# Moving all GpSimd arithmetic of a fused attention and two-layer kernel to VectorE

## The chip, the cores and the metric

One core of one Trainium2 chip runs the whole program. The metric is device time in microseconds (us) of one execution, the median of three runs. Times of single instructions and waits come from one profiled execution.

## The reference

Everything is float32. Three stages follow each other.

```python
# 1 attention, q, k, v: 4 batches, 8 heads, 576 positions, 64 wide
q_d, k_d, v_d = means over groups of 4 positions            # 144 positions
out_up = repeat(softmax(q_d k_d^T / 8) v_d, 4)
out_local = softmax(where(|i - j| < 4, q k^T / 8, -1e9)) v   # a narrow band
x = (out_up + out_local)  as 2304 tokens x 512
# 2 first gated layer, 512 -> 1536 -> 512
x = ((x @ w_a) * (x @ w_b)) @ w_out
# 3 second gated layer, 512 -> 2048 -> 512
h = x @ w_in
x = (h * clip(h + 3, 0, 6) / 6) @ w_out2
```

The softmax sums have 1e-9 added before the division.

## The kernel before

The weights arrive as 64-bit words, and the kernel turns each word into float32 itself. `decode` (line 229) does that for one tile of 128 x 1024 words in a buffer `raw`: ScalarE takes a magnitude (L243), VectorE runs six instructions (L249, L250, L254, L260, L261, L267), and then the value is split into a coarse part and a remainder, so that TensorE can multiply in three passes (`PASSES`) in its quick format. The coarse part is ScalarE's copy (`first`, L271). The remainder is a subtraction (`second`, L275), on VectorE where `soon` is set (the first three tiles of the first layer's weights), else on GpSimd. There are 12 tiles `wab` (first layer, w_a and w_b together), 6 tiles `wo`, 8 tiles `w2i` and 8 tiles `w2o`. Two `raw` buffers exist, and the subtraction frees one for the next load.

`pieces` (line 292) decodes a `w2i` tile, forms seven combinations of its quarters (L308), copies each to its place (L317) and subtracts (L321). Its flag `soon` is set for tiles 5 to 7. For tiles 0 to 4 GpSimd subtracts.

The attention goes in two forms. `pooled` (line 361) takes one pair of heads of one batch: sums of four positions of q and k (VectorE, L391), sums of v (`add_v`, L386 and L387, on GpSimd), scores (TensorE, L400), maxima (VectorE, L405 and L408), exponentials with their sums (ScalarE, L414), reciprocals (VectorE, L420 and L421), the normalisation (`scaled`, L353), a transposition (TensorE, L432) and the product with v (L447). `local` (line 470) takes one unit of 116 tokens and all heads of a batch in the same steps (L487/L493, L501/L502, L509, L514/L515, L353, L524, L536), adds the two results (VectorE, L544) and splits x into coarse part and remainder (ScalarE L551, VectorE L554). The normalisation L353 is VectorE's for block 0 (the flag `first`, `m < 1`) and GpSimd's for all else.

The 20 units form seven blocks of tokens (`BLOCKS`). `job` (line 562) multiplies one block with one `wab` tile: 12 matmuls for a, 12 for b (L586), ScalarE copies a out of PSUM (L592), VectorE multiplies by b (L595), and SyncE stores to DRAM (L598). There are 84 jobs. Then come the second product of layer one (`second`, L643, with h loaded, copied at L631 and subtracted at L635), and layer two (`inner`, L755; `outer`, L878).

Nothing is put in order by hand. `Plan` keeps a list of steps with engine, estimated length, the time at which each is wanted, dependencies and buffers taken and given, walks through them as a clock would, and writes each instruction when its engine is free, its inputs are there and its buffers are free; of several, the one wanted first. So each engine's queue is fixed when the program is written, and an engine that waits for one instruction holds up all behind it. A step's engine and length (lines 185 to 202) decide where everything else lands.

Of the kernel before, what the change touches and what calls it, by code (L numbers as in the profile page):

```python
# [138 lines left out]
def fused_kernel(ctx: ExitStack, tc: tile.TileContext, qk, vt, vd, wab, wo, w2i, w2o, mask, out):  # L139
# [54 lines left out]
    def act(n):  # L194
        return 0.1 + 0.00095 * n

    def pool(n):
        return 0.2 + 0.0023 * n

    def dma(kb):  # L200
        return 0.0039 * kb

# [8 lines left out]
    def DVE(busy, want, run, after=(), take=(), give=(), slack=0.0):  # L211
        return plan.add("DVE", busy, want, run, after, take, give, DVE_L + slack)

    def POOL(busy, want, run, after=(), take=(), give=(), slack=0.0):
        return plan.add("POOL", busy, want, run, after, take, give, DVE_L + slack)

    issued = {}

    def DMA(kb, want, run, after=(), take=(), give=()):
# [6 lines left out]
    wab_t, wo_t, w2_t = {}, {}, {}  # L226
    pools = {}

    def decode(src, want, put, tag, after=(), ahead=4, soon=False, slack=1.0, raw=None, queue=None):

        T = {}

        def load():
            T["raw"] = slot(xp if raw == "x" else dp, [P, W], mybir.dt.uint64, raw or "raw", "raw")
            (queue or nc.sync).dma_start(T["raw"], src)

        def words():
            w = T["raw"].bitcast(U32).rearrange("p (n t) -> p n t", t=2)
            return w[:, :, 0], w[:, :, 1]

        def magnitude():
            T["m"] = slot(dp, [P, W], F32, "dm", "m")
            nc.scalar.activation(T["m"], words()[1].bitcast(F32), AF.Abs)  # L243

        def exponent():
            m = T["m"]
            mu = m.bitcast(U32)

            nc.vector.tensor_scalar(m, m, W_MIN, W_MAX, op0=ALU.max, op1=ALU.min)  # L249
            nc.vector.tensor_scalar(mu, mu, 3, 0x3FFFFFF8, op0=ALU.logical_shift_left, op1=ALU.bitwise_and)  # L250

        def upper():
            hi = words()[1]
            nc.vector.scalar_tensor_tensor(out=hi, in0=hi, scalar=0xC0000000, in1=T["m"].bitcast(U32),  # L254
                                           op0=ALU.bitwise_and, op1=ALU.bitwise_or)

        def lower():
            m, (lo, hi) = T["m"], words()

            nc.vector.tensor_scalar(m.bitcast(U32), hi, 0xFF800000, None, op0=ALU.bitwise_and)  # L260
            nc.vector.scalar_tensor_tensor(out=lo.bitcast(F32), in0=lo, scalar=2.0 ** -52, in1=m,  # L261
                                           op0=ALU.mult, op1=ALU.mult)

        def both():
            lo, hi = words()
            v = hi.bitcast(F32)
            nc.vector.tensor_tensor(v, v, lo.bitcast(F32), op=ALU.add)  # L267

        def first():
            T["w"] = put()  # L270
            nc.scalar.activation(T["w"][:, 0], words()[1].bitcast(F32), AF.Copy)  # L271

        def second():
            eng = nc.vector if soon else nc.gpsimd
            eng.tensor_tensor(T["w"][:, 1], words()[1].bitcast(F32), T["w"][:, 0], op=ALU.subtract)  # L275


        i = DMA(1024, want - ahead, load, take=[raw or "raw"])
        i = ACT(act(W), want, magnitude, [i], take=["dm"], slack=slack)
        i = DVE(2 * dve2(W), want, exponent, [i])  # L280
        i = DVE(dve(W), want, upper, [i])
        i = DVE(dve2(W) + dve(W), want, lower, [i], give=["dm"])
        if put is None:
            return DVE(dve(W), want, both, [i], slack=slack), words
        i = DVE(dve(W), want, both, [i], slack=slack)
        i = ACT(act(W), want, first, [i, *after], take=[tag], slack=slack)
        return (DVE(dve(W), want, second, [i], give=[raw or "raw"]) if soon else
                POOL(pool(W), want, second, [i], give=[raw or "raw"]))

    takers = {}  # L290

    def pieces(src, want, where, soon, raw=None):


        i, words = decode(src, want, None, None, slack=1.0, raw=raw)
# [17 lines left out]
        for at, of, q, n in ((0, 0, 0, 2), (2, 0, 3, 1), (3, 1, 0, 4)):  # L313
            for a, b, key, tag, before, place in where(at, at + n):
# [3 lines left out]

                def second(a=a, b=b, of=of, q=q + a - at, place=place):
                    x = quarters()[of][:, q:q + b - a]  # L320
                    (nc.vector if soon else nc.gpsimd).tensor_tensor(place(1), x, place(0), op=ALU.subtract)  # L321

                n_ = (b - a) * Q
                j = ACT(act(n_), want, first, [i, *before, takers.get(key)], take=[tag] if tag else [], slack=1.0)
                takers.setdefault(key, j)
                ends.append(DVE(dve(n_), want, second, [j]) if soon else POOL(pool(n_), want, second, [j]))
        return plan.add("-", 0, want, lambda: None, ends, give=[raw or "raw"])


# [18 lines left out]
    ods, xs, qks = {}, {}, {}  # L348
    S_ = {}

    def scaled(eng, e, z):

        eng.tensor_tensor(e, e, z.unsqueeze(2).to_broadcast(list(e.shape)), op=ALU.mult)  # L353

    def two_banks(name):
        return slot(ps, [P, 2, BANK], F32, "s2", name)
# [1 line left out]
    def one_bank(name):  # L358
        return slot(ps, [P, BANK], F32, "b", name)

    def pooled(b, g, want, first):

        T = {}

# [18 lines left out]
        def add_v():  # L383
            v_ = T["v_"]
            T["v"] = v_[:, :, 0] if b == 0 else slot(ap, [HD, 2, P], F32, "dv", "dv")
            nc.gpsimd.tensor_tensor(v_[:, :, 0:2], v_[:, :, 0:2], v_[:, :, 2:4], op=ALU.add)  # L386
            nc.gpsimd.tensor_tensor(T["v"], v_[:, :, 0], v_[:, :, 1], op=ALU.add)  # L387

        def sums():
            T["s"] = slot(ap, [P, 2, SD], F32, "dqk", "dqk")  # L390
# [30 lines left out]
            nc.vector.reciprocal(z, z)  # L421

        def norm():
            scaled(nc.vector if first else nc.gpsimd, T["e"], T["z"])

        def turn(c):
            def run():
# [26 lines left out]
        early = want - 30 if b == 0 else want - 6  # L454
        ld = S_["qk", b, g] = DMA(590, early + 0.1 * g, load, take=["wh" if b == 0 else "qk"])
        lv = DMA(290, early + 1 + 0.1 * g, load_v, take=["wh" if b == 0 else "vraw"])
        av = POOL(pool(768), want - 3, add_v, [lv], take=[] if b == 0 else ["dv"], give=[] if b == 0 else ["vraw"])
        i = DVE(dve(2 * S), want, sums, [ld], take=["dqk"])
        S_["sums", b, g] = i
        i = PE(0.5, want, score, [i], take=["s2"], give=["dqk"])  # L460
        i = DVE(dve(4 * SD) + 0.16, want, top, [i])
        i = ACT(4 * 0.47, want, exps, [i], take=["de"], give=["s2"])
        i = DVE(0.32, want, inverse, [i])
        i = DVE(dve(4 * SD), want, norm, [i]) if first else POOL(pool(4 * SD), want, norm, [i])
        t = [PE(0.3, want, turn(c), [i], take=["b", "turn"], give=["de"] if c else []) for c in range(2)]
# [4 lines left out]
    def local(u, want, first):  # L470

        L = {}
        b, j = divmod(u, NU)
# [41 lines left out]
            nc.vector.reciprocal(z, z)  # L515

        def norm():
            scaled(nc.vector if first else nc.gpsimd, L["e"].rearrange("q p h k -> q (p h) k"),
                   L["z"].rearrange("q p h -> q (p h)"))

        def turn():
# [40 lines left out]
        i = DVE(dve(n) + 0.2, want, top, [i], give=[])  # L562
        i = ACT(8 * 0.42, want, exps, [i], take=["e"], give=["s2"])
        i = DVE(0.36, want, inverse, [i])
        i = DVE(dve(n), want, norm, [i]) if first else POOL(pool(n), want, norm, [i])
        i = PE(0.5, want, turn, [i], take=["b", "turn"], give=["e"])
        i = ACT(act(n), want, turned, [i], take=["eT"], give=["b", "turn"])
        i = S_["pv", u] = PE(0.9, want, pv, [i, ld], take=["b", "pv"], give=["eT"])
# [374 lines left out]
    for u in place:  # L943
# [2 lines left out]
        t = when[m, 0] - 4 + 0.1 * i if m < 3 else T1 - 30 + 4 * i if m == 3 else T1 - 14 + 1.25 * (i + 3 * m - 12)  # L946
        if u % NU == 0:
            for g in range(HP):
                pooled(u // NU, g, t - 0.05 + 0.01 * g, m < 1)
        local(u, t, m < 1)  # L950
    for f in range(F1):
        S_["wab", f] = decode(wab[f], when[0, f] - 4, lambda f=f: wab_t.setdefault(f, slot(wpool, [P, 2, W], F32R, "wh", "wh")),
                              "wh", ahead=26 if f < 2 else 6, soon=f < 3, slack=0.0,
                                queue=nc.scalar if f < 2 else None)
    for t, (n, f) in enumerate(jobs):
        job(n, f, t, n == NBLK - 1)
# [52 lines left out]
    for i in range(F2 // 2):  # L1009
        if i == 5:  # L1010
            S_["p3"] = plan.add("-", 0, 0, open_p3, [S_["h", n, f] for n, f in jobs[-2:]] + [S_["raw x", k] for k in SPARE])
        S_["raw x", i] = pieces(w2i[i], T1 + 8 + 5.5 * i, place_of(i), i > 4, "x" if i in SPARE else None)
        S_["w2i", i] = S_["raw x", i]


# [146 lines left out]
```

## Time and profile before

| | us |
|---|---|
| median of 3 runs (989.52 to 989.85) | 989.83 |
| the profiled execution, its own device time | 986.13 |
| its span, first to last instruction | 984.3 |
| TensorE (PE) busy | 929.0 |
| VectorE (DVE) busy | 754.6 |
| ScalarE (ACT) busy | 455.4 |
| GpSimd (POOL) busy | 146.3 |

An engine's busy time counts overlapping instructions once. TensorE is busy for 94% of the span, but not evenly: the stretches of the first rows below show where it waits. TensorE's clock has two levels, 2.4 and 1.2 GHz; the column PEclk gives the granted clock as a mean share of the full one.

### The profile page before, as it was taken

To read this page: it belongs to the slowest core of one execution; us is meant where nothing else is said; L and a number is where in the kernel's file an instruction comes from. 1 tells how busy PE (TensorE), PEld (TensorE's weight loads), DVE (VectorE), ACT (ScalarE), POOL (GpSimd) and SP (SyncE) were. 2 spreads that over 40 slices of the span, in tenths; PEclk is the share of its full clock that TensorE was granted. 3 is DMA by queue.
4 is the path that set the end of the run, shared out by engine and by line. 5 is a ranking of instruction groups with operands and counts; after the bars stand their busy time and mean duration, and the time that the engine had idled before them with its cause. 6 is when DMAs were issued, how large, how long until landed. Compare 5 with 4: busy or idle time off the path is not lost.

```text
span 984.3 us, 18584 instructions
## 1 busy us (share of the span) xinstructions
PE 929.0 (94%) x7040; PEld 869.2 (88%) x7040; DVE 754.6 (77%) x1293; ACT 455.4 (46%) x1164; POOL 146.3 (15%) x141
## 2 busy tenths in 40 slices
PE   4789988999999989999999999999999999999998
PEld 2568978899899989998777788899999999999998
DVE  6986999742624969597678754799988999997883
ACT  3766544342556323232344333445544655554551
POOL 5236144240212323331000000000000000000000
PEclk9988999999999999999999999999999999999999
DMA  9443544422404343314687874244327882714401
GB/s 271 159 131 129 171 172 146 163 80 64 145 33 145 119 172 129 129 44 144 215 267 233 285 254 148 85 151 159 139 91 250 275 286 65 255 52 160 162 18 49
DMA packets 90089, 151.21 MB, mean 154 GB/s; under 512 B 8208, under 2 KB 71696, under 8 KB 85648
## 3 DMA queue, kind: packets, MB, share of 16 engines
q1 hardware_dynamic: 80384, 132.54, 40.8%
q10 hardware_dynamic: 9616, 17.49, 5.6%
q8 instruction: 55, 0.90, 0.4%
q14 instruction: 34, 0.28, 0.1%
HBM read 100.19 MB, written 49.81 MB: 152 GB/s over the span
## 4 chain that ended last, share of the span: by engine, by line
PE 64%; DVE 22%; DMA 7%; issue 4%; ACT 2%; POOL 0%; SPq 0%; ACTq 0%; DVEq 0%
PE ph L755 18%; PE pab L586 16%; PE oacc L878 15%; PE acc L643 10%; DMA h<-h_d 3%; DVE raw L254 3%; DVE m L249 2%; DVE m L260 2%; DVE raw L261 2%; DVE m L250 2%; PE po L536 2%; DVE a L595 2%; DVE raw L267 2%; DVE in L686 1%; DMA qk<-qk 1%
## 5 line engine op out<-in xcount | busy, mean ns | idle before, releaser
L586 PE MATMUL pab<-x,wh 128*128 128x344 f32 (+2 forms) x2016 | 328.3, 322 | 14.5 <-ACT a L592 7.3
L586 PEld LDWEIGHTS pab<-x,wh 128*128 128x128 f32 x2016 | 313.5, 193 | 19.7 <-ACT a L592 8.6
L878 PE MATMUL oacc<-w2o,in 128*128 128x256 f32 x1512 | 181.8, 283 | 1.4 <-DVE in L686 1.4
L878 PEld LDWEIGHTS oacc<-w2o,in 128*128 128x128 f32 x1512 | 181.3, 191 | 2.0 <-DVE in L686 1.8
L755 PE MATMUL ph<-in,w 128*128 128x384 f32 x1008 | 175.7, 335 | 2.2 <-ACT in L683 2.0
L755 PEld LDWEIGHTS ph<-in,w 128*128 128x128 f32 x1008 | 175.2, 188 | 2.6 <-ACT in L683 2.2
L643 PE MATMUL acc<-h,wo 128*128 128x512 f32 (+1 forms) x720 | 155.3, 375 | 7.2 <-ACT h L631 4.7
L643 PEld LDWEIGHTS acc<-h,wo 128*128 128x128 f32 x720 | 125.9, 190 | 36.6 <-ACT h L631 6.7
L595 DVE TENSOR_TENSOR a<-a,pab 128x344 f32<-128x344 f32 (+2 forms) x84 | 41.2, 493 | 76.1 <-PE pab L586 57.3
L771 DVE TENSOR_TENSOR part<-ph,part 128x384 f32<-128x384 f32 x168 | 85.9, 551 | 9.1 <-PE ph L755 8.4
L779 ACT ACTIVATE r<-part,three 128x384 f32<-128x384 f32 x96 | 56.4, 613 | 54.5 <-DVE part L771 52.0
L635 DVE TENSOR_TENSOR h<-h 128x512 fp32r<-128x512 f32 (+1 forms) x60 | 37.6, 635 | 48.7 <-ACT h L631 48.4
L243 ACT ACTIVATE m<-raw 128x1024 f32<-128x1024 f32 x34 | 39.0, 1148 | 67.7 <-DVE raw L261 35.6
L592 ACT ACTIVATE a<-pab 128x344 f32<-128x344 f32 (+2 forms) x84 | 36.5, 446 | 71.7 <-PE pab L586 47.4
L683 ACT ACTIVATE in<-gr 128x384 fp32r<-128x384 f32 x96 | 47.5, 521 | 41.2 <-PE oacc L878 29.0
L631 ACT ACTIVATE h<-h 128x512 fp32r<-128x512 f32 (+1 forms) x60 | 34.7, 589 | 56.4 <-DMA h<-h_d 47.0
L686 DVE TENSOR_TENSOR in<-gr,in 128x384 fp32r<-128x384 f32 x96 | 49.6, 553 | 6.6 <-ACT in L683 5.9
L509 ACT ACTIVATE e<-sc,mx 128x64 f32<-128x64 f32 x160 | 47.6, 327 | 11.4 <-DVE mx L502 10.0
L683 ACT ACTIVATE in<-e 128x384 fp32r<-128x384 f32 x72 | 36.5, 526 | 33.9 <-PE oacc L878 21.9
L782 DVE SCALAR_TENSOR_TENSOR r<-r,part 128x384 f32<-128x384 f32 x96 | 50.5, 551 | 1.1 <-ACT r L779 1.1
L254 DVE SCALAR_TENSOR_TENSOR raw<-raw,m 128x1024 uint32<-128x1024 uint32 x34 | 49.7, 1461 | 0.9
L261 DVE SCALAR_TENSOR_TENSOR raw<-raw,m 128x1024 f32<-128x1024 uint32 x34 | 42.6, 1252 | 1.2
(86 smaller groups left out, 1002.0 us busy)
## 6 DMA issues: line engine op xcount, KB each, us to landing
g_d<-r SPq DMA_DIRECT2D x96, 192.0 KB, 1.9
gr<-g_d SPq DMA_DIRECT2D x48, 384.0 KB, 4.1
h<-h_d ACTq DMA_DIRECT2D x48, 256.0 KB, 2.9
raw<-wab SPq DMA_DIRECT2D x10, 1024.0 KB, 6.0
h_d<-a SPq DMA_DIRECT2D x48, 172.0 KB, 1.8
raw<-w2i SPq DMA_DIRECT2D x8, 1024.0 KB, 6.2
raw<-w2o SPq DMA_DIRECT2D x8, 1024.0 KB, 6.2
qk<-qk SPq DMA_DIRECT2D x14, 576.0 KB, 4.7
```

The source lines that it names most:

```text
L254: nc.vector.scalar_tensor_tensor(out=hi, in0=hi, scalar=0xC0000000, in1=T["m"].bitcast(U32), op0=ALU.bitwise_and, op1=ALU.bitwise_or)
L261: nc.vector.scalar_tensor_tensor(out=lo.bitcast(F32), in0=lo, scalar=2.0 ** -52, in1=m, op0=ALU.mult, op1=ALU.mult)
L586: nc.tensor.matmul(T[k], wab_t[f][:, x, c], xs[n][:, g, y, :nb], start=(g == 0 and i == 0), stop=(g == KC - 1 and i == 2))
L595: nc.vector.tensor_tensor(T["a"], T["a"], T[1], op=ALU.mult)
L643: nc.tensor.matmul(accs[n][e], wo_t[f // 2][:, x, c], hs[n, f][:, y], start=(f == 0 and i == 0), stop=(f == F1 - 1 and i == 2))
L683: nc.scalar.activation(x[0][:, 0], src(), AF.Copy)
L686: nc.vector.tensor_tensor(x[0][:, 1], src(), x[0][:, 0], op=ALU.subtract)
L755: nc.tensor.matmul(acc[k], t[:, x, g * P:(g + 1) * P], X[k, g][0][:, y], start=(g == 0 and n == 0), stop=(g == 1 and n == 2))
L771: nc.vector.tensor_tensor(s[name], acc[k], s[other], op=ALU.add)
L779: nc.scalar.activation(T["r"], src(), AF.Relu, bias=three)
L782: nc.vector.scalar_tensor_tensor(out=T["r"], in0=T["r"], scalar=6.0, in1=src(), op0=ALU.min, op1=ALU.mult)
L878: nc.tensor.matmul(acc[n][e], X[n, k][0][:, x, e * P:(e + 1) * P], t[:, y], start=(k == 0 and i == 0), stop=(k == K - 1 and i == 2))
```

## The change

GpSimd keeps its memsets and loses all arithmetic: the subtraction that ends `decode` (L275), the one of `pieces` (L321), the two additions of `add_v` (L386, L387) and the normalisations (L353) are VectorE's for every tile and unit. The flags `soon` and `first`, the estimate `pool` and the function `POOL` go, and `Plan` counts these steps as VectorE's with VectorE's lengths, so that the order of all engines comes out anew. Later lines stand up to 8 lower in the changed file.

```diff
-            eng = nc.vector if soon else nc.gpsimd
-            eng.tensor_tensor(T["w"][:, 1], words()[1].bitcast(F32), T["w"][:, 0], op=ALU.subtract)
+            nc.vector.tensor_tensor(T["w"][:, 1], words()[1].bitcast(F32), T["w"][:, 0], op=ALU.subtract)
...
-        return (DVE(dve(W), want, second, [i], give=[raw or "raw"]) if soon else
-                POOL(pool(W), want, second, [i], give=[raw or "raw"]))
+        return DVE(dve(W), want, second, [i], give=[raw or "raw"])
...
-                    (nc.vector if soon else nc.gpsimd).tensor_tensor(place(1), x, place(0), op=ALU.subtract)
+                    nc.vector.tensor_tensor(place(1), x, place(0), op=ALU.subtract)
...
-                ends.append(DVE(dve(n_), want, second, [j]) if soon else POOL(pool(n_), want, second, [j]))
+                ends.append(DVE(dve(n_), want, second, [j]))
...
-    def scaled(eng, e, z):
+    def scaled(e, z):
...
-        eng.tensor_tensor(e, e, z.unsqueeze(2).to_broadcast(list(e.shape)), op=ALU.mult)
+        nc.vector.tensor_tensor(e, e, z.unsqueeze(2).to_broadcast(list(e.shape)), op=ALU.mult)
...
-            nc.gpsimd.tensor_tensor(v_[:, :, 0:2], v_[:, :, 0:2], v_[:, :, 2:4], op=ALU.add)
-            nc.gpsimd.tensor_tensor(T["v"], v_[:, :, 0], v_[:, :, 1], op=ALU.add)
+            nc.vector.tensor_tensor(v_[:, :, 0:2], v_[:, :, 0:2], v_[:, :, 2:4], op=ALU.add)
+            nc.vector.tensor_tensor(T["v"], v_[:, :, 0], v_[:, :, 1], op=ALU.add)
...
-        av = POOL(pool(768), want - 3, add_v, [lv], take=[] if b == 0 else ["dv"], give=[] if b == 0 else ["vraw"])
+        av = DVE(dve(768) + 0.06, want - 3, add_v, [lv], take=[] if b == 0 else ["dv"], give=[] if b == 0 else ["vraw"])
...
-        i = DVE(dve(4 * SD), want, norm, [i]) if first else POOL(pool(4 * SD), want, norm, [i])
+        i = DVE(dve(4 * SD), want, norm, [i])
...
-        i = DVE(dve(n), want, norm, [i]) if first else POOL(pool(n), want, norm, [i])
+        i = DVE(dve(n), want, norm, [i])
```

How VectorE's queue changes is seen at three places. The first is the start of the program, where the pooled attention of batch 0 begins (`dqk` are sums of q and k, `v_...` the four tiles of v, `de` exponentials, `dz` their sums, `dmx` maxima). VectorE before:

```order
L391 TENSOR_REDUCE dqk<-qk_132 128x288
L353 TENSOR_TENSOR de<-de,dz 72x576
L405 TENSOR_REDUCE dmx<-dsc 72x4
L408 TENSOR_SCALAR dmx<-dmx 72x4
L420 TENSOR_SCALAR dz<-dz 72x4
```

VectorE in the changed kernel, from the same sum on:

```order
L383 TENSOR_REDUCE dqk<-qk_132 128x288
L378 TENSOR_TENSOR v_146<-v_146 72x2x256
L379 TENSOR_TENSOR v_146<-v_146 72x2x128
L378 TENSOR_TENSOR v_156<-v_156 72x2x256
L379 TENSOR_TENSOR v_156<-v_156 72x2x128
L345 TENSOR_TENSOR de<-de,dz 72x576
L378 TENSOR_TENSOR v_161<-v_161 72x2x256
L379 TENSOR_TENSOR v_161<-v_161 72x2x128
L378 TENSOR_TENSOR v_178<-v_178 72x2x256
L379 TENSOR_TENSOR v_178<-v_178 72x2x128
```

The eight sums of v stand ahead of the first normalisation and of the third maximum, which had VectorE to themselves.

The second place is the decoding of a `wab` tile (`raw`, `m`) between jobs (`a<-a,pab`), after the eighth job product. VectorE before:

```order
L249 TENSOR_SCALAR m<-m 128x1024
L250 TENSOR_SCALAR m<-m 128x1024
L254 SCALAR_TENSOR_TENSOR raw<-raw,m 128x1024
L595 TENSOR_TENSOR a<-a,pab 128x348
L260 TENSOR_SCALAR m<-raw 128x1024
L261 SCALAR_TENSOR_TENSOR raw<-raw,m 128x1024
```

VectorE in the changed kernel, where `wh` is a finished tile and `e` a unit's exponentials:

```order
L268 TENSOR_TENSOR wh<-raw,wh 128x1024
L243 TENSOR_SCALAR m<-m 128x1024
L244 TENSOR_SCALAR m<-m 128x1024
L345 TENSOR_TENSOR e<-e,z 128x512
L248 SCALAR_TENSOR_TENSOR raw<-raw,m 128x1024
L345 TENSOR_TENSOR e<-e,z 128x512
L254 TENSOR_SCALAR m<-raw 128x1024
L255 SCALAR_TENSOR_TENSOR raw<-raw,m 128x1024
```

The subtraction that ends the tile before and two normalisations stand between the decoding instructions.

The third place is the first `w2i` tile (`w_...` are the places of its pieces, `wo` a tile of the second product). VectorE before:

```order
L308 TENSOR_TENSOR raw<-raw 128x256 x4
L249 TENSOR_SCALAR m<-m 128x1024
L250 TENSOR_SCALAR m<-m 128x1024
L254 SCALAR_TENSOR_TENSOR raw<-raw,m 128x1024
L260 TENSOR_SCALAR m<-raw 128x1024
```

VectorE in the changed kernel, from the same combinations on:

```order
L300 TENSOR_TENSOR raw<-raw 128x256 x4
L587 TENSOR_TENSOR a<-a,pab 128x344
L248 SCALAR_TENSOR_TENSOR raw<-raw,m 128x1024
L587 TENSOR_TENSOR a<-a,pab 128x348
L254 TENSOR_SCALAR m<-raw 128x1024
L255 SCALAR_TENSOR_TENSOR raw<-raw,m 128x1024
L313 TENSOR_TENSOR w_4070<-raw,w_4070 128x2x256
L313 TENSOR_TENSOR w_4073<-raw,w_4073 128x3x256
L313 TENSOR_TENSOR w_4070<-raw,w_4070 128x256 x2
L261 TENSOR_TENSOR raw<-raw 128x1024
```

The four subtractions of the tile's pieces stand inside the decoding of the next tile, ahead of its last instruction.

## Rows read from the trace of the kernel before

**Rows 1.** Busy time of each engine in six stretches, with granted clock and DMA.
```profile
core 0: us, PE busy (x) PEld busy (x) DVE busy (x) ACT busy (x) POOL busy (x), PEclk, DMA share, GB/s
0.00:58.00 58.00, 35.20 (x404) 26.43 (x405) 46.26 (x72) 31.85 (x139) 22.31 (x45) 0.94 0.70 218
58.00:110.00 52.00, 48.88 (x612) 42.93 (x610) 39.90 (x64) 31.75 (x115) 22.44 (x18) 0.90 0.35 109
110.00:190.00 80.00, 71.85 (x616) 68.47 (x612) 72.65 (x93) 34.31 (x110) 28.61 (x21) 1.00 0.50 169
190.00:318.00 128.00, 126.58 (x1352) 117.10 (x1353) 55.02 (x109) 62.03 (x257) 29.12 (x32) 0.99 0.30 96
318.00:461.00 143.00, 136.36 (x837) 134.01 (x836) 113.51 (x131) 44.19 (x72) 43.79 (x25) 0.99 0.35 118
461.00:984.30 523.30, 510.10 (x3231) 480.26 (x3229) 427.22 (x827) 251.28 (x476) 0.00 (x0) 1.00 0.52 172
```

**Rows 2.** PE waits from 110 to 190 us: who, for whom, us, times, longest.
```profile
PE pab L586 <- ACT a L592: 2.6, 2, 1.7
PE dpt L432 <- ACT a L592: 1.2, 1, 1.2
```

**Rows 3.** PE waits from 318 to 461 us.
```profile
PE pab L586 <- DVE a L595: 3.1, 3, 2.1
PE pab L586 <- ACT a L592: 2.5, 2, 1.5
```

**Rows 4.** Groups of GpSimd instructions: count, busy us, mean ns, idle before.
```profile
L321 POOL TENSOR_TENSOR w<-raw,w 128x256 fp32r<-128x256 f32 (+3 forms) x20 | 30.9, 1568 | 53.7 <-ACT w L317 53.7
L275 POOL TENSOR_TENSOR wh<-raw,wh 128x1024 fp32r<-128x1024 f32 x9 | 22.4, 2484 | 22.1 <-ACT wh L271 22.1
L353 POOL TENSOR_TENSOR e<-e,z 128x512 f32<-128x512 f32 x18 | 21.1, 1170 | 65.4 <-DVE z L515 65.4
L386 POOL TENSOR_TENSOR vraw<-vraw 72x512 f32<-72x512 f32 x12 | 17.3, 1442 | 27.1 <-DMA vraw<-vd 27.1
L353 POOL TENSOR_TENSOR de<-de,dz 72x576 f32<-72x576 f32 x12 | 16.8, 1397 | 37.4 <-DVE dz L421 35.4 <-ACT od L452 2.0
```

**Rows 5.** Groups of DVE instructions from 461 us on, to 622 us.
```profile
L254 DVE SCALAR_TENSOR_TENSOR raw<-raw,m 128x1024 uint32<-128x1024 uint32 x9 | 11.0, 1222 | 0.1
...
L250 DVE TENSOR_SCALAR m<-m 128x1024 uint32<-128x1024 uint32 x9 | 6.2, 694 | 0.3
...
L249 DVE TENSOR_SCALAR m<-m 128x1024 f32<-128x1024 f32 x9 | 6.2, 687 | 0.0
...
L321 DVE TENSOR_TENSOR w<-raw,w 128x512 fp32r<-128x512 f32 x4 | 2.7, 682 | 0.0
L321 DVE TENSOR_TENSOR w<-raw,w 128x256 fp32r<-128x256 f32 x6 | 2.3, 417 | 0.0
L321 DVE TENSOR_TENSOR w<-raw,w 128x1024 fp32r<-128x1024 f32 x1 | 1.2, 1216 | 0.0
```

**Rows 6.** Timeline around 111 us: start us, us, engine, line, operation.
```profile
110.25 2.93 POOL L275 TENSOR_TENSOR wh<-raw,wh 128x1024 fp32r<-128x1024 f32 x1 [0.32 <-ACT wh L271]
...
110.91 2.91 DVE L250 TENSOR_SCALAR m<-m 128x1024 uint32<-128x1024 uint32 x1
...
113.75 0.67 DVE L501 TENSOR_REDUCE mx<-sc 128x8 f32<-128x512 f32 x1
```

**Rows 7.** Groups of DVE instructions from 0 to 461 us.
```profile
L254 DVE SCALAR_TENSOR_TENSOR raw<-raw,m 128x1024 uint32<-128x1024 uint32 x25 | 38.7, 1547 | 0.8
...
L250 DVE TENSOR_SCALAR m<-m 128x1024 uint32<-128x1024 uint32 x25 | 24.7, 986 | 0.9
L249 DVE TENSOR_SCALAR m<-m 128x1024 f32<-128x1024 f32 x25 | 24.4, 977 | 12.1 <-ACT m L243 12.1
...
L260 DVE TENSOR_SCALAR m<-raw 128x1024 uint32<-128x1024 uint32 x25 | 23.1, 924 | 0.4
```

**Rows 8.** Timeline of DVE: first and last of 58 stretched instructions.
```profile
13.19 0.50 DVE L408 TENSOR_SCALAR dmx<-dmx 72x4 f32<-72x4 f32 x1
...
445.66 1.33 DVE L267 TENSOR_TENSOR raw<-raw 128x1024 f32<-128x1024 f32 x1
```

More of the change, by code (lines that the diff above doesn't have):

```diff
@@ L195, in act @@
         return 0.1 + 0.00095 * n
-    def pool(n):
-        return 0.2 + 0.0023 * n
     def dma(kb):
@@ L212, in DVE @@
         return plan.add("DVE", busy, want, run, after, take, give, DVE_L + slack)
-    def POOL(busy, want, run, after=(), take=(), give=(), slack=0.0):
-        return plan.add("POOL", busy, want, run, after, take, give, DVE_L + slack)
     issued = {}
@@ L227, in fused_kernel, with decode @@
     pools = {}
-    def decode(src, want, put, tag, after=(), ahead=4, soon=False, slack=1.0, raw=None, queue=None):
+    def decode(src, want, put, tag, after=(), ahead=4, slack=1.0, raw=None, queue=None):
         T = {}
@@ L286, in decode, with pieces @@
         i = ACT(act(W), want, first, [i, *after], take=[tag], slack=slack)
-        return (DVE(dve(W), want, second, [i], give=[raw or "raw"]) if soon else
-                POOL(pool(W), want, second, [i], give=[raw or "raw"]))
+        return DVE(dve(W), want, second, [i], give=[raw or "raw"])
     takers = {}
-    def pieces(src, want, where, soon, raw=None):
+    def pieces(src, want, where, raw=None):
         i, words = decode(src, want, None, None, slack=1.0, raw=raw)
@@ L359, in one_bank, with pooled @@
         return slot(ps, [P, BANK], F32, "b", name)
-    def pooled(b, g, want, first):
+    def pooled(b, g, want):
         T = {}
@@ L423, in norm @@
         def norm():
-            scaled(nc.vector if first else nc.gpsimd, T["e"], T["z"])
+            scaled(T["e"], T["z"])
         def turn(c):
@@ L468, in pooled, with local @@
         S_["od", b, g] = ACT(act(SD), want, keep, [i, S_.get(("od", b, 0))], take=[] if g else ["od"], give=["b", "pv"])
-    def local(u, want, first):
+    def local(u, want):
         L = {}
@@ L517, in norm @@
         def norm():
-            scaled(nc.vector if first else nc.gpsimd, L["e"].rearrange("q p h k -> q (p h) k"),
+            scaled(L["e"].rearrange("q p h k -> q (p h) k"),
                    L["z"].rearrange("q p h -> q (p h)"))
@@ L948, in fused_kernel @@
             for g in range(HP):
-                pooled(u // NU, g, t - 0.05 + 0.01 * g, m < 1)
-        local(u, t, m < 1)
+                pooled(u // NU, g, t - 0.05 + 0.01 * g)
+        local(u, t)
     for f in range(F1):
         S_["wab", f] = decode(wab[f], when[0, f] - 4, lambda f=f: wab_t.setdefault(f, slot(wpool, [P, 2, W], F32R, "wh", "wh")),
-                              "wh", ahead=26 if f < 2 else 6, soon=f < 3, slack=0.0,
+                              "wh", ahead=26 if f < 2 else 6, slack=0.0,
                                 queue=nc.scalar if f < 2 else None)
@@ L1011, in fused_kernel @@
             S_["p3"] = plan.add("-", 0, 0, open_p3, [S_["h", n, f] for n, f in jobs[-2:]] + [S_["raw x", k] for k in SPARE])
-        S_["raw x", i] = pieces(w2i[i], T1 + 8 + 5.5 * i, place_of(i), i > 4, "x" if i in SPARE else None)
+        S_["raw x", i] = pieces(w2i[i], T1 + 8 + 5.5 * i, place_of(i), "x" if i in SPARE else None)
         S_["w2i", i] = S_["raw x", i]
```

## The prediction

> **What bounds the kernel now.** I cut the span into stretches first, since the shares over the whole of it hide where TensorE waits. In the six stretches [rows 1] the reader is to compare TensorE's busy time with the length. From 461 us to the end TensorE is busy for 510.1 of 523.3 us and GpSimd does nothing: the change moves no work there, and that part can only shift as a whole. From 190 to 318 us TensorE misses 1.4 us, so nothing can be won, and VectorE is free for 73 of 128 us, so much can be added. Three stretches remain. Up to 58 us TensorE has 22.8 us free, as it waits for first loads and for the first attention. From 110 to 190 us it misses 8.2 us while VectorE is busy for 72.7 of 80. From 318 to 461 us it misses 6.6 us while VectorE is busy for 113.5 of 143.
>
> Then I asked what those pauses wait for, in the list of waits. Both times it is mostly the emptying of PSUM for a job: ScalarE's copy a and VectorE's product a, which stand in their queues behind other work. The two largest waits are 2.6 and 1.2 us in the earlier stretch [rows 2], 3.1 and 2.5 us in the later [rows 3]. So these two stretches depend on how fast VectorE's queue moves, through VectorE itself and through ScalarE, which waits for VectorE's results.
>
> **What is moved.** The groups of GpSimd's instructions [rows 4] give the counts. There are 9 subtractions of `wab` tiles and 6 of `wo` tiles (all six, by the code), 18 normalisations of 512 elements, 12 of 576, 20 subtractions of pieces, and 16 pairs of additions for v (12 of these first additions have their row, four more write in place for batch 0, and each has a second addition of half the size). That is 97 instructions.
>
> VectorE's price for the same operation stands in a stretch without GpSimd [rows 5]: 1.216 us for 1024 elements, 0.682 for 512, 0.417 for 256. On that line 576 elements cost 0.75 and 768 cost 0.95. The pieces are ten of 256, six of 512, three of 768 and one of 1024 (7 x 256 elements a tile, five tiles). So: 15 x 1.216 = 18.2; 18 x 0.682 = 12.3; 12 x 0.75 = 9.0; 16 x (0.682 + 0.417) = 17.6; pieces 4.2 + 4.1 + 2.9 + 1.2 = 12.4. Together 69.5 us by recorded lengths. A VectorE instruction starts before the recorded end of the one ahead: in [rows 6] L250 ends at 110.91 + 2.91 = 113.82 and L501 starts at 113.75. That is 0.07 us each, 97 x 0.07 = 6.8, which leaves **62.7 us added**. The additions over 72 partitions do not occur on VectorE before; I take them at the price by length. Their bounds are the same pair at 512 and 256 elements without the overlap, 1.10 us, and one single instruction of 512, 0.68; over 16 pairs that is 3 us on VectorE either way, which does not decide anything.
>
> **What is removed.** The row that matters most is L250 at 110.91 us [rows 6]. It took 2.91 us, where its mean in the stretch without GpSimd is 0.694 [rows 5]. A GpSimd subtraction ran from 110.25 to 113.18, and L250 ended 0.64 us later: it stood still until GpSimd was done. The groups show this as a habit. Up to 461 us the means are 1547, 986, 977 and 924 ns for L254, L250, L249 and L260 [rows 7]; after it L254, L250 and L249 take 1222, 694 and 687 [rows 5], and I take L250's 694 for L260. Over 25 each that is 8.1 + 7.3 + 7.3 + 5.8 = 28.5 us lost on these four lines. Worked out the same way for every VectorE instruction that overlaps GpSimd arithmetic, against the median of its own kind without overlap, the loss is **51.3 us**, in 58 instructions of which the first and last have rows [rows 8]. It falls into the stretches as 6.0, 5.1, 13.0, 4.9 and 22.3 us.
>
> So VectorE's load rises by only 62.7 - 51.3 = 11.4 us, and where it rises decides. I counted in the two orders how many moved instructions stand ahead of the 8th, 24th and 48th job product (110, 190 and 311 us before). A 1024 costs 1.15 net of overlap, a pair 0.96, a 576 0.68, a 512 0.61.
>
> Up to 110 us: 11 pairs, 4 + 6 normalisations, 1 subtraction: 10.6 + 2.7 + 3.7 + 1.2 = 18.2 us; removed 11.1; net +7.1. The new order also pulls some 2 us of maxima and of one x remainder ahead: +9.
>
> From 110 to 190 us: 7 subtractions and 2 normalisations, 9.3 us; removed 13.0; net -3.7. Besides, sums and maxima of the next attention move behind this stretch.
>
> From 190 to 318 us: 17.5 us; removed 4.9; net +12.6, into VectorE's 73 free us. It costs nothing; were that cover gone, it would be 12.6 us.
>
> From 318 to 461 us: 6 subtractions and 20 pieces, 6.9 + 11.0 = 17.9 us; removed 22.3; net -4.4.
>
> **What of it reaches the end.** In the two stretches where TensorE waits for VectorE's queue, VectorE gets 8 us lighter, and its longest instruction falls from some 3 to 1.2 us, so a job's product no longer stands behind a stalled decoding step. The subtraction also ends a tile sooner: 1.22 us in place of 2.48 [rows 4, 5]. Of TensorE's 8.2 + 6.6 = 14.8 us I take half as won, **-7.4 us**, as part of each pause is the queue's fixed order, which stays whatever the lengths. The bounds are 0 (all of it order) and -14.8.
>
> In the first 110 us VectorE gets 9 us heavier, and has 11.7 + 12.1 = 23.8 us free, part of it the first loads. At the start it now does eight additions, 4 us, ahead of the third maximum, against about 3.5 us of stalls that go there. What queues behind is the pooled attention, ScalarE's exponentials behind its maxima, and the second `wab` load, issued from ScalarE's queue. I put **+1.5 us** on this stretch, between -1 and +9. GpSimd's memsets no longer wait behind arithmetic, which lets loads of q and k start sooner; TensorE is not waiting for these after 58 us, so nothing.
>
> Half speed is a separate term. The granted clock is 0.90 from 58 to 110 us [rows 1], so about a tenth of twice 52, 10.4 us, went at 1.2 GHz, after pauses at the start; it costs about 5 us. I leave it as it is: bounds 5 us either way.
>
> The sum: -7.4 + 1.5 = -5.9 us on the profiled execution, 986.1 to 980.2. The median of the runs shown lies 3.7 us above that execution, so I forecast **984 us**.
>
> A rule of the Trainium skill speaks against the change: its page "Perfetto Trace Analysis", section "Optimizing Scalar/DVE Operations", says that where VectorE is saturated it may pay to hand work to GpSimd, though it adds that the two share a port and that this might not help. By its first half alone nothing would be removed and the stretch from 110 to 190 us would grow by 9.3 us, to about 999 in all. The trace bears out its second half here: 51.3 of 62.7 us come back.
>
> **The rivals.**
>
> *No change.* TensorE's pauses come from the order alone: a job's product waits where the plan put it, whatever the lengths. For it: in each stretch part of the waits is for ScalarE's copy, which GpSimd does not stall directly. Against it: the plan before knew nothing of 51 us of stalls and so drifted from what the chip did; the new plan counts every moved step. It gives 988 to 992.
>
> *Slower: VectorE becomes the bound before 110 us.* Place: the attention of batches 0 and 1 and the first four tiles. VectorE takes 9 us more there, and this reaches TensorE if VectorE's free time cannot be filled, because it is spent waiting for TensorE and ScalarE within the same chain. The point from which it decides: more than about half of the 12.1 free us from 58 to 110 must stay unusable. If none is usable and nothing is regained later, 989.8 + 9 = 999; with part regained, 993 to 997.
>
> *More than half won.* All 14.8 us go and some half-speed time with them: 989.8 - 14.8 - 5 + 1.5 = 971.5; as a case, 968 to 978.
>
> That GpSimd keeps some arithmetic can be left out: in the new order only memsets stand on it.
>
> **How the numbers follow.** The forecast, 978 to 988, gets 0.50; more won, 0.12; no change, 0.17; slower, 0.21. A measurement tells about 0.2% (2 us) from no change, so faster means below 987.8. Nearly all of the forecast and all of "more won" lie there, 0.62; same 0.17; slower 0.21. For the range I cut the far ends of both outer cases, about a tenth each: 974 to 995; the likeliest case alone has 978 to 988.
>
> **What would show it.** VectorE's L249, L250, L254 and L260 must all be near 0.69 and 1.22 us on average over the whole run; if they stay long, the stall is not GpSimd's. VectorE's busy time should rise by about 11 us, to some 766. TensorE's waits for L592 and L595 should shrink in the stretches that answer to 110 to 190 and 318 to 461 us, and the 24th job product should come some 2 to 5 us earlier than the 188 us of before. The eighth should come within 2 us of 110; if it comes 5 or more later, the slower rival holds. From the end of the jobs on, everything should be as before, only shifted. The forecast is wrong if the new order makes new pauses of TensorE behind VectorE's longer queue, above all in the first 110 us.

## The result and the profile after

The changed kernel takes 974.84 us (median, 972.43 to 976.37); the kernel before took 989.67 us beside it. The ratio is 0.9859, 95% interval 0.9822 to 0.9895: 1.4% faster. The profiled execution took 975.95 us, its span is 974.2 us. Forecast were 984 us, with a range of 974 to 995; the likeliest case alone had 978 to 988, so the change won more than the likeliest case allowed. It lies 0.84 us inside the lower end of the range, less than the changed kernel's own runs differ by (972.43 to 976.37): that the range still holds it is luck.

Busy time of each engine in the changed kernel, in the same stretches and columns as [rows 1]:

```profile
0.00:58.00 58.00, 33.47 (x390) 24.46 (x392) 45.16 (x81) 31.22 (x137) 3.97 (x28) 0.94 0.69 214
58.00:110.00 52.00, 47.12 (x575) 41.68 (x576) 45.90 (x87) 34.06 (x146) 0.64 (x8) 0.90 0.39 119
110.00:190.00 80.00, 79.84 (x636) 78.10 (x634) 73.11 (x101) 31.20 (x58) 0.00 (x0) 1.00 0.55 180
190.00:318.00 128.00, 128.00 (x1433) 117.34 (x1430) 73.79 (x150) 67.47 (x281) 0.64 (x8) 1.00 0.31 96
318.00:461.00 143.00, 142.99 (x864) 139.00 (x863) 109.16 (x165) 48.64 (x80) 0.00 (x0) 1.00 0.41 143
461.00:974.20 513.20, 496.31 (x3159) 469.16 (x3157) 418.83 (x809) 244.74 (x464) 0.00 (x0) 0.99 0.51 166
```

From 110 to 461 us TensorE's pauses are gone: 0.2 us are missing in 351, where 16.2 were before. Up to 110 us TensorE is busy 3.5 us less than before. The list of TensorE's waits, where [rows 2] had L592 at the head, has one row from 110 to 190 us and none from 318 to 461:

```profile
PE pab L578 <- DVE x L546: 0.2, 1, 0.2
```

VectorE's groups over the whole run (count, busy us, mean ns, idle before). These are the lines L254, L250, L260 and L249 of [rows 7], with their new numbers L248, L244, L254 and L243:

```profile
L248 DVE SCALAR_TENSOR_TENSOR raw<-raw,m 128x1024 uint32<-128x1024 uint32 x34 | 41.5, 1220 | 0.2
L244 DVE TENSOR_SCALAR m<-m 128x1024 uint32<-128x1024 uint32 x34 | 23.6, 694 | 1.2
L254 DVE TENSOR_SCALAR m<-raw 128x1024 uint32<-128x1024 uint32 x34 | 23.4, 687 | 0.4
L243 DVE TENSOR_SCALAR m<-m 128x1024 f32<-128x1024 f32 x34 | 23.3, 686 | 5.8 <-ACT m L237 5.8
```

The stalls are gone. The page gives VectorE's busy time as:

```profile
PE 927.7 (95%) x7040; PEld 869.7 (89%) x7040; DVE 766.0 (79%) x1390; ACT 457.3 (47%) x1164; POOL 5.2 (1%) x44
```

That is the 766 forecast. So the account of VectorE's load came out as worked out, while the time fell by 14.8 us where 5.9 were forecast.

### The profile page after: what moved, and what is told of

Same layout as the page of the kernel before. It is cut to its first block, busy times and chain, and to the rows that moved or that the text cites. A ratio compares the mean times of both kernels' runs of the same rounds, so it can differ in the third digit from the quotient of the medians.

```text
span 974.2 us, 18526 instructions
## 1 busy us (share of the span) xinstructions
PE 927.7 (95%) x7040; PEld 869.7 (89%) x7040; DVE 766.0 (79%) x1390; ACT 457.3 (47%) x1164; POOL 5.2 (1%) x44
## 4 chain that ended last, share of the span: by engine, by line
PE 80%; DVE 9%; DMA 7%; ACT 2%; issue 2%; ACTq 0%; SPq 0%; DVEq 0%
PE pab L578 32%; PE ph L747 16%; PE oacc L870 15%; PE acc L635 9%; DMA h<-h_d 4%; PE po L528 2%; DVE in L678 2%; DMA vz<-vt 1%; PE sc L485 1%; PE pt L516 1%; PE dpo L439 1%; DVE e L843 1%; DVE w2o L1078 1%; PE dpt L424 1%; DMA raw<-wab 1%
## 5 line engine op out<-in xcount | busy, mean ns | idle before, releaser
L584 ACT ACTIVATE a<-pab 128x344 f32<-128x344 f32 (+2 forms) x84 | 37.3, 447 | 95.8 <-PE pab L578 67.5
L627 DVE TENSOR_TENSOR h<-h 128x512 fp32r<-128x512 f32 (+1 forms) x60 | 37.4, 634 | 51.6 <-ACT h L623 51.3
L261 DVE TENSOR_TENSOR raw<-raw 128x1024 f32<-128x1024 f32 x34 | 41.5, 1221 | 0.5
```

## The experiments

All times are in us. A stretch runs from one job product's end to another's (the 8th, 24th, 48th and 84th product on L595); in brackets stands TensorE's idle time in it, its length less its busy time. The last column is how long ScalarE waited from 110 to 190 us with `wh` L271 at the head of its queue for VectorE's L267 (the two steps and L595 have other line numbers in some of the kernels). The ratio is to runs of the kernel before beside it, whose median was 986.97 to 989.67, so kernels are compared by their ratios rather than their medians. Stretches come from one trace each, and part of a length is the clock, which stood at 1.2 GHz for 3.4 to 23.9 us up to the 84th product; the idle times in brackets say more than the lengths.

| kernel | median | ratio, 95% interval | to 8th | 8 to 24 | 24 to 48 | 48 to 84 | L271 waits |
|---|---|---|---|---|---|---|---|
| before (its trace) | 989.83 | | 109.7 (25.9) | 78.1 (7.3) | 123.3 (2.3) | 149.4 (6.6) | 31.7 |
| changed | 974.84 | 0.9822 to 0.9895 | 115.1 (29.6) | 61.0 (0) | 126.2 (0) | 140.1 (0) | 14.5 |
| e1_order_alone | 975.91 | 0.984 to 0.9923 | 108.1 (27.3) | 65.7 (2.5) | 126.0 (0) | 142.9 (1.5) | 12.8 |
| e2_engine_alone | 980.22 | 0.9891 to 0.9947 | 112.4 (29.2) | 75.8 (6.5) | 122.2 (0) | 138.8 (0) | 26.5 |
| e3_weights_alone | 967.37 | 0.9757 to 0.9861 | 105.1 (24.6) | 65.3 (0) | 122.0 (0) | 143.3 (1.6) | 11.0 |
| e4_attention_alone | 986.8 | 0.9969 to 1.0012 | 114.0 (28.7) | 65.8 (2.2) | 125.4 (1.5) | 149.2 (5.2) | 22.0 |
| e5_before_deferred | 990.78 | 1.0021 to 1.007 | 106.0 (22.8) | 75.3 (5.2) | 126.6 (4.4) | 149.7 (3.9) | 27.7 |
| e6_weights_and_norms | 974.37 | 0.9825 to 0.9908 | 115.4 (29.2) | 66.6 (0.3) | 120.9 (0) | 140.1 (0) | 13.1 |
| e7_weights_deferred | 967.82 | 0.9764 to 0.9844 | 108.4 (23.5) | 63.9 (0) | 125.4 (0) | 139.9 (0) | 10.6 |
| e9_changed_x_loads_late | 974.66 | 0.9842 to 0.9924 | 109.7 (28.5) | 61.3 (0) | 126.2 (0) | 140.1 (0) | 13.4 |
| e10_before_again | 990.95 | 0.9995 to 1.0039 | 108.8 (24.1) | 79.6 (6.9) | 122.0 (1.5) | 148.6 (5.8) | 29.5 |
| e11_plan_books_stalls | 967.03 | 0.9724 to 0.9824 | 109.9 (25.5) | 70.1 (2.0) | 119.9 (0) | 141.3 (0.8) | 20.9 |
| e12_weights_order_alone | 980.11 | 0.9886 to 0.995 | 105.0 (22.2) | 68.3 (1.8) | 122.2 (1.3) | 150.3 (5.2) | 13.0 |
| e14_plan_books_scalar | 984.07 | 0.9937 to 0.9974 | 112.0 (29.0) | 72.1 (4.6) | 121.5 (0) | 147.8 (4.9) | 14.1 |

**The new order without the new engine, and the other way round.** `e1_order_alone` is the changed kernel, whose plan still counts every moved step as VectorE's, with the instructions issued where before had them, here at one of five places:

```diff
-                    nc.vector.tensor_tensor(place(1), x, place(0), op=ALU.subtract)
+                    (nc.vector if soon else nc.gpsimd).tensor_tensor(place(1), x, place(0), op=ALU.subtract)
```

> The order of the changed kernel, as its plan makes it, but each moved instruction is issued on GpSimd wherever it was GpSimd's before. Stall theory (the time lies in VectorE standing still while GpSimd computes): some 50 us of VectorE's time go back into stalls, in an order that leaves no room for them, so 984 to 995 us. Order theory (the new order alone brings the gain, since the plan counts the steps better): VectorE is relieved of 63 us and the order is kept, so 970 to 979 us.

`e2_engine_alone` is the kernel before with its order, and VectorE issues:

```diff
-            scaled(nc.vector if first else nc.gpsimd, T["e"], T["z"])
+            scaled(nc.vector, T["e"], T["z"])
```

> The order of the kernel before, planned as if the 97 instructions were GpSimd's, but each is issued on VectorE. Stall theory: the stalls are gone and 63 us of work are added at places where the plan saw none, net +11 us on VectorE, so most of the gain is there: 974 to 981 us. Order theory: 987 to 996 us.

By its time `e1_order_alone` lies where the theory of the order put it, and `e2_engine_alone` where the theory of the stalls did: neither theory is the whole. The order alone has the whole gain, although VectorE loses 51.3 us to stalls in it, as before. The engine alone has 0.8%, nearly all of it behind the 48th product. The largest item of TensorE's waits from 110 to 190 us in `e2_engine_alone`, without a single stall:

```profile
PE pab L586 <- ACT a L592: 4.1, 2, 2.3
```

So in the earlier stretch a removal of the stalls leaves the waits, though this kernel also does added work at places where its plan counted none. The new order leaves 2.5 of 7.3 us of them with the stalls kept, and a third order with all stalls, `e11_plan_books_stalls` below, leaves 2.0: the waits are mostly the order's. From 318 us on either repair takes most of them away, and the two gains don't add.

**Which of the moved steps.** `e3_weights_alone` moves L275 and L321 only, `e4_attention_alone` the sums of v and the normalisations only, each in the plan as well. One place of each:

```diff
-        return (DVE(dve(W), want, second, [i], give=[raw or "raw"]) if soon else
-                POOL(pool(W), want, second, [i], give=[raw or "raw"]))
+        return DVE(dve(W), want, second, [i], give=[raw or "raw"])
```

```diff
-        i = DVE(dve(4 * SD), want, norm, [i]) if first else POOL(pool(4 * SD), want, norm, [i])
+        i = DVE(dve(4 * SD), want, norm, [i])
```

> Only the subtractions of weights and pieces (35 instructions) are VectorE's, planned so; normalisations and sums of v stay GpSimd's. Stall theory: the stretches of the first 9 tiles and of the second product's tiles and pieces win, the first 110 us stay as before (no 5 us lost at the eighth product), the attention's stalls stay: 975 to 981 us. If the attention's stalls are what counts: 985 to 990 us.

> Only normalisations and sums of v (62 instructions) are VectorE's, planned so; subtractions of weights and pieces stay GpSimd's. Stall theory: the first 110 us lose some 5 us as in the changed kernel, little comes back between 190 and 318 us, and from 318 us all stalls are as before: 987 to 994 us. If the attention's stalls are what counts: 975 to 981 us.

The subtractions alone, at 967.37 us, came out below both expectations, and by the median below the whole change, though the intervals of the two overlap. Their trace reaches the 84th product 6.7 us sooner than the changed kernel's, but it also spent 3.4 us at 1.2 GHz up to there, the changed kernel 17.1, and at half speed that difference alone is 6.8 us. The attention's part alone is worth nothing that can be measured (0.9969 to 1.0012). `e6_weights_and_norms` is `e3_weights_alone` with the normalisations on VectorE too (the second diff), the sums of v left on GpSimd:

> As in the changed kernel but the sums of v stay on GpSimd. If the sums of v are what delays the first eight job products by 5 us, the eighth comes 3 to 5 us sooner than the changed kernel's, and the whole takes 969 to 973 us. If it is the normalisations, the eighth stays where it was in the changed kernel (about 115 us) and the whole at 973 to 977 us. Load theory for the stretch after it: VectorE's work by the order is 66 us there, 9 more than in the changed kernel, so that stretch takes about 70 us, and part of the gain goes.

It comes out like the whole change, so the sums of v cost nothing that can be measured. By the medians it costs 7 us against `e3_weights_alone`, which would be the normalisations with the order they bring, but the two intervals overlap. Its first eight products come 10.3 us later than those of `e3_weights_alone`: its trace records 820 matmuls and transpositions of the attention ahead of them, 778 there, and it stood at 1.2 GHz for 20.5 us up to the 84th product against 3.4; its idle time up to the eighth is 4.6 us longer. Of its expectation for the next stretch, 70 us, it had 66.6.

**Less load on VectorE.** `e5_before_deferred` holds the sums, the sums of v and the scores of batch 2 back until the tenth `wab` tile is decoded; `e7_weights_deferred` does so in `e3_weights_alone`, until the last tile is. In both the tiles are also listed ahead of the attention, which can settle ties in the plan.

```diff
-        i = DVE(dve(2 * S), want, sums, [ld], take=["dqk"])
+        i = DVE(dve(2 * S), want, sums, [ld, S_["wab", 9] if b == 2 else None], take=["dqk"])
```

> The kernel before, GpSimd keeps all its arithmetic; alone the attention of batch 2 (its sums, its scores) may not begin before the 10th of the 12 first-layer tiles is decoded. Load theory (between the 8th and the 24th job product VectorE is the bound, and the stretch is as long as VectorE's own work in it plus some 5 us; the new order wins by moving attention out of it): VectorE has some 9 us less there with the stalls kept, so 66 to 69 us in place of 78, and 977 to 982 us in all. Stall theory (only GpSimd's stalls count): no change, 986 to 991 us.

> Only the subtractions of weights and pieces are VectorE's, and besides the attention of batch 2 may not begin before the 12th first-layer tile is decoded. Load theory: VectorE's work from the 8th to the 24th job product falls from 61 to 55 us, the stretch from 65 to about 60; TensorE is the bound after it and half of this is lost again, so 962 to 967 us. Stall theory: as with the subtractions alone, 966 to 969 us.

The theory of the load fell: VectorE's busy time between the 8th and the 24th product went from 71.8 to 61.9 us, TensorE still waited 5.2 us, and the time was 990.78 us, as the other theory had it. In the second kernel the hold changed nothing that can be measured.

**What the plan counts.** What is common to the good orders is that the plan gives VectorE time for the steps. `e11_plan_books_stalls` tests just that. Nothing is moved: it is the kernel before with two lines in the plan's loop, where a step has been placed.

```diff
                     free[engine] = now + busy
+                    if engine == "POOL":
+                        free["DVE"] = max(free["DVE"], now) + 0.36 * busy
```

> The kernel before, every instruction on its engine as before; only the plan, when it places a step on GpSimd, also books 0.36 of its length on VectorE (51.2 us of stalls over 143 us of GpSimd arithmetic). Theory that the order is good where the plan counts VectorE's lost time: from the 8th to the 24th product 64 to 68 us (78.1 before) with at most 2.5 us of waits of TensorE, time 974 to 981. Rival, that the order is good because the subtraction or normalisation itself is a step in VectorE's queue: 74 to 79 us, 5 us of waits or more, time 985 to 991.

967.03 us, 2.3% faster than before, with every instruction on its old engine. No kernel run has a lower median, though `e3_weights_alone` (967.37) and `e7_weights_deferred` (967.82) can't be told from it. VectorE stalls as much as before (54.2 us up to the 84th product, worked out as for [rows 8]). L254 and L250, which are L256 and L252 here, have 1630 and 1038 ns in the stretch of [rows 7], and TensorE's waits from 110 to 190 us have shrunk to one row, which is not a job's:

```profile
L256 DVE SCALAR_TENSOR_TENSOR raw<-raw,m 128x1024 uint32<-128x1024 uint32 x25 | 40.7, 1630 | 0.6
```

```profile
PE dpo L449 <- ACT deT L441: 2.0, 1, 2.0
```

The stretch from the 8th to the 24th product, 70.1 us, lies between the two expectations, but 6.9 us of it went at 1.2 GHz (166.2 to 173.1 us), and none in the first trace of before; without these 3.4 us it is within the first. TensorE's 2.0 us of waits are as the first had them, and the time is better than it had. The trace ends 7.3 us ahead of the changed kernel's: 1.3 us of that are there at the 84th product, 5.1 come in the second product, which took 160.0 us in place of 165.1. VectorE's order differs there throughout, so this lead is not shown to come from the stalls' booking. `e14_plan_books_scalar` is the control, with `"ACT"` for `"DVE"` in the added lines:

> A control for the plan that booked GpSimd's stalls: the kernel before, every instruction on its engine as before; when the plan places a step on GpSimd, it books the same 0.36 of its length, but on ScalarE, which does not lose it. If the gain of 22 us came from counting VectorE's lost time, this order is no better than before: 984 to 992, with 5 us or more of TensorE's waits from the 8th to the 24th product. If any shake of the order frees it from an unlucky one, it gains too: 967 to 980.

It gains 0.4%, some 4.5 of 22 us: the first expectation had the time at its edge (984.07) and the waits nearly (4.6 us, not 5), the second only the sign. So a shake of the order may give a little, and TensorE's waits for VectorE's product stay, as in [rows 3], from 318 to 461 us:

```profile
PE pab L588 <- DVE a L597: 4.7, 3, 3.0
```

`e12_weights_order_alone` is `e3_weights_alone` with both subtractions issued by GpSimd as before:

> The order of the kernel in which only the subtractions of tiles and pieces are VectorE's, but GpSimd issues them as before, so that some 50 us of stalls stay. If a good order hides the stalls (as the order of the whole change did): 966 to 971, as with the subtractions on VectorE (967.4). If the stalls' removal adds to the order: 974 to 981, and the TensorE waits from the 8th to the 24th and from the 48th to the 84th product are 5 us or more together.

It stands 12.7 us above `e3_weights_alone`, as its second expectation had it, and the two intervals do not overlap: here GpSimd's issuing does cost, by its stalls or by subtractions that end later (2.48 us in place of 1.22 for a tile), which no run parts. 7.0 us are among the last products, where TensorE waits 5.2 us, and 3.0 between the 8th and the 24th. In the order of the whole change it costs 1.1 us (`e1_order_alone`), within its uncertainty. So the cost depends on the order, on what it has put behind a stalled or late step.

**The second product.** In the changed kernel it gave back a part: from the 84th product to the last of its 720 matmuls it took 165.1 us, 159.3 before. `e9_changed_x_loads_late` holds the loads of x for layer two back, which went out beside a slow load of h: TensorE waited 4.4 us for it. `e10_before_again` is the kernel before once more.

```diff
-            return DMA(NB, want - 12 if p else want - 6, run, S_["x2d", m[t]] + ([] if p == 0 else [opened]),
+            return DMA(NB, want - 12 if p else want - 6, run, S_["x2d", m[t]] + ([S_["second", 3, 8]] if p == 0 else [opened]),
```

> The changed kernel, but the four loads of x for the first pair of layer two may not begin before the 45th of the 60 steps of the second product. If these loads (1.5 MB) slow the loads of h, so that TensorE waits 4.4 us and its clock falls at 543 us, that wait shrinks to under 2 us and the whole to 968 to 973 us. If the loads and stores of w2o do it, nothing changes: 973 to 977 us.

> The kernel before, unchanged, to have a second trace of it. If the changed kernel itself loses the time in the second product of layer one (from the 84th job product to the last of the 720 matmuls: 159.3 us in the first trace of before, 165.1 in the changed kernel), this stretch takes 158 to 161 us again. If it is spread between executions, since the queues' order there is the same in both, it takes 163 to 167. Theory of the order: TensorE's waits from the 8th to the 24th product are 5 us or more again. Time 985 to 991 either way.

Of `e10_before_again` the waits (6.9 us) and the time came as expected, but neither expectation on the second product held: 162.4 us lies between them. The thirteen traces other than the first of before have 160.0 to 167.6. The same queues had 159.3 and 162.4, and `e5_before_deferred`, whose order of that product differs from before only in its first two dozen VectorE instructions, 165.8. So 3 us of spread are there without any change and 6 with hardly one, and the 5.8 can't be put down to the change. The late loads left the longest of these waits at 3.1 us, not under 2, and gave 1.2 us in the trace and nothing in the time.

## Why the prediction was right and wrong

**VectorE's account held.** 0.69 and 1.22 us on the four decoding lines, 766.0 us busy, no stall left. The prices of the moved steps were right as well:

```profile
L268 DVE TENSOR_TENSOR wh<-raw,wh 128x1024 fp32r<-128x1024 f32 x12 | 14.6, 1214 | 2.1 <-ACT wh L265 2.1
L345 DVE TENSOR_TENSOR e<-e,z 128x512 f32<-128x512 f32 x20 | 13.7, 684 | 0.2
L378 DVE TENSOR_TENSOR vraw<-vraw 72x512 f32<-72x512 f32 x12 | 8.1, 678 | 3.4 <-DMA vraw<-vd 3.4
```

The additions over 72 partitions, which had only bounds, cost the price by length. One reading of the lines is off: what the prediction calls the two largest waits in [rows 2] and [rows 3] are totals of one to three waits each, the longest 2.1 us. Nothing in its sum hangs on it.

**The step that failed** is "Of TensorE's 8.2 + 6.6 = 14.8 us I take half as won, -7.4 us, as part of each pause is the queue's fixed order, which stays whatever the lengths". All of it was won: in these two stretches, 110 to 190 and 318 to 461 us, 0.2 us are left, and from the 8th to the 84th product TensorE's idle time fell from 16.2 us to nothing. That term was 7.4 us too small, and the reason given was wrong in its second half. The order is not fixed, since the change alters the plan's lengths, and the new order alone removes most of the waits while the stalls stay (`e1_order_alone`: 4.0 us left). The mechanism on which the sum rested, that a job's product no longer stands behind a stalled step, fits from the 48th product on (`e2_engine_alone`: 6.6 us of idle time to 0, though its subtractions also end sooner) but gives almost nothing between the 8th and the 24th (7.3 to 6.5). What the rival "no change" named, a product that "waits where the plan put it", was the mover, only with the other sign.

What that looks like in the queue, from `e10_before_again`. These are VectorE's and ScalarE's timelines (start us, us, line, idle before) around TensorE's wait at 192 us:

```profile
181.56 2.00 DVE L249 TENSOR_SCALAR m<-m 128x1024 f32<-128x1024 f32 x1 [1.92 <-ACT m L243]
...
188.24 1.22 DVE L267 TENSOR_TENSOR raw<-raw 128x1024 f32<-128x1024 f32 x1
```

```profile
189.49 1.15 ACT L271 ACTIVATE wh<-raw 128x1024 fp32r<-128x1024 f32 x1 [7.27 <-DVE raw L267]
190.55 1.11 ACT L243 ACTIVATE m<-raw 128x1024 f32<-128x1024 f32 x1
191.56 0.34 ACT L592 ACTIVATE a<-pab 128x232 f32<-128x232 f32 x1
```

```profile
168.51 20.86 PE L586 MATMUL pab<-x,wh 128*128 128x344 f32 x144 [0.51 <-ACT a L592]
...
191.96 2.15 PE L586 MATMUL pab<-x,wh 128*128 128x344 f32 x12 [1.48 <-ACT a L592]
```

L249 took 2.00 us, 0.69 without a stall. L271 stands ahead of a job's copy L592, and ScalarE stood 7.27 us at L271. My reading is that the plan, which has no stalls in its books, expected L267 earlier than it came; `e11_plan_books_stalls` fits it, but no run shows when the plan expected it. TensorE had finished its matmuls of the jobs at 189.37 (168.51 + 20.86), and the job's copy, which empties their PSUM, came only at 191.56, behind L271 and L243. In the changed kernel ScalarE waits at that step half as long in all (14.5 us from 110 to 190, 29.5 in `e10_before_again`), and around the same time the job's copy L584 stands where it waits for a store of its own, not for decoding:

```profile
187.28 0.36 ACT L584 ACTIVATE a<-pab 128x232 f32<-128x232 f32 x1 [0.93 <-DMA h_d<-a]
```

By itself the total is no measure: `e14_plan_books_scalar` has 14.1 us of it, and TensorE still idles for 4.6. It costs only where something that TensorE needs stands behind it. In `e14_plan_books_scalar` 4.2 of the 4.6 us have another path: TensorE waits for ScalarE's split of x, that for VectorE's sum `xf`, and this stands in VectorE's queue directly behind a decoding step (L252) that took 2.86 us beside GpSimd, 0.69 without.

**The 24th product**, forecast 2 to 5 us earlier, came 11.7 earlier, although the eighth came 5.3 later: the stretch between them is 17.1 us shorter. 7.3 us of that are the idle time that went. The other 9.8 are no gain by themselves: the prediction saw that "sums and maxima of the next attention move behind this stretch" and gave it no price. Between the 8th and the 24th product the trace records 72 matmuls and transpositions of the attention, 162 before; it has 26 more from the 24th to the 48th, where the changed kernel is 2.9 us longer, and 56 more from the 48th to the 84th.

**The first 110 us**, "+1.5 us, between -1 and +9": the eighth product came 5.3 us later, which is the mark set for the slower rival, and that did not follow, as it was regained behind it. TensorE's idle time there grew by 3.7 us; in `e9_changed_x_loads_late`, with the same order up to there, it grew by 2.6, and the eighth product came when it did before. I can't assign the rest; the clock fell to 1.2 GHz at other places, which differ between executions. The direction was right and the size within its bounds. There is a new pause of the kind that the prediction feared, "behind VectorE's longer queue": at 52 us the transposition of a unit waits for its normalisation, which before was GpSimd's. TensorE's wait for it up to 110 us, before and in the changed kernel (us, times, longest):

```profile
PE pt L524 <- POOL e L353: 0.5, 1, 0.5
```

```profile
PE pt L516 <- DVE e L345: 3.4, 1, 3.4
```

`e6_weights_and_norms` has it too (3.8 us), `e3_weights_alone` does not. This points to the normalisations as the cause, not to the eight sums of v that the prediction pointed at; the order has a part in it, as `e1_order_alone` waits 2.3 us there with GpSimd issuing.

**The clock, "I leave it as it is"**: up to the 84th product 23.9 us went at 1.2 GHz before, of which the prediction counted 10.4, and 17.1 in the changed kernel; at half speed the difference is 3.4 us, within the 5 us of its bounds. Up to 110 us both have 17. What went are the two stretches of before behind that, 191.0 to 194.4 and 358.2 to 361.7 us, each right behind a pause of TensorE (2.3 and 2.1 us) that is gone in the changed kernel. So a part of the clock's cost went with the pauses, as the rival "more than half won" had it.

**"Everything should be as before, only shifted" from the end of the jobs on**: the 84th product came 18.1 us earlier, the end 10.2 (984.3 to 974.2). 5.8 of the 7.9 us between fall into the second product, within the spread above; 2.0 come behind it, where the traces of all kernels spread by 2.2.

So up to the 84th product: idle time +3.7 - 16.2 = -12.5, clock -3.4, and 2.2 us that I can't assign: -18.1. What came is the rival "more than half won", 968 to 978, to which the prediction gave 0.12; it named the size and the clock, but not that the new order does it.

What stays open: why `e14_plan_books_scalar` gains 0.4% although what it books is lost nowhere; why GpSimd's issuing costs 12.7 us in one order and 1.1 in another; whether the booking on VectorE must stand beside GpSimd's steps, or any spare time in VectorE's plan would do, which no run tested; and whether the two best edits, subtractions on VectorE and a plan that books the remaining stalls, add up, which was not run.

## What to carry to other kernels

Where a planner fixes the queues from estimated lengths, a change of an estimate moves more than the instruction it stands for: split such a change into the order alone and the engine alone before giving either the credit. Time that one engine costs another belongs in the planner's books; two lines that book it won at least as much here as moving all of the work. When TensorE waits for a copy, look at what the copying engine was standing at.

## What the runs showed of the hardware

VectorE's decoding steps stood still while GpSimd computed, but not every VectorE instruction did, and ScalarE's did not. In the trace of before the product L595 (128x344) took 0.508 us alone and 0.512 beside GpSimd's arithmetic, and ScalarE's copy L592 of the same size 0.458 either way. The product lost nothing itself; it was late through what stood ahead of it.

Two executions of the unchanged kernel, with the same queues, differ by some 3 us in one stretch: the second product took 159.3 us in the first trace and 162.4 in the second. The clock was at 1.2 GHz at other places, among them 51.0 to 57.9 and 71.5 to 81.8 us in the first, 74.2 to 81.0 and 156.1 to 163.0 in the second. A difference of a few us between single traces is no evidence by itself. A single load can be slow: the load of h that TensorE waited for from 538.9 us in the changed kernel took 8.48 us, the one ahead of it 4.65.
